# A gated mix of two S4 layers on one Trainium2 core: the last unit transposed on VectorE, one product per step in place of two, and a new written-out order

## The chip, the cores and the metric

The program runs on one core of a Trainium2 chip. The metric is device time in microseconds: the median of the runs shown. A core has four engines that compute, each with its own queue of instructions that it works off strictly in the order of the program: TensorE (PE in the profile, with PEld for the loading of its weights), VectorE (DVE), ScalarE (ACT) and GpSimd (POOL). SyncE (SP) issues all transfers of this kernel. [...] PSUM is the memory that TensorE writes its products to; SBUF holds everything else.

## The reference

Two state-space layers (A, "S4", and B, "S4D") see the same input `x` of 2048 steps by 512 channels. Each builds a convolution kernel of 2048 taps per channel from 128 complex exponentials, convolves the input with it through a Fourier transform of length 4096, and adds a skip term. A sigmoid gate, one number per step, mixes the two.

```python
x = A_u
g = _sigmoid((x * gate_w).sum(-1, keepdims=True))
# each layer: K[d,l] = Re sum_n C[d,n] * exp(dt*A[d,n]*l) * B[d,n]   (512 x 2048, 128 terms)
#             y = irfft(rfft(x, 4096) * rfft(K, 4096))[:2048] + x * Dskip
a = _A_ref(x, A_A_re, A_A_im, A_B_re, A_B_im, A_C_re, A_C_im, A_log_dt, A_Dskip)
b = _B_ref(x, B_log_A_real, B_A_imag, B_C_real, B_C_imag, B_log_dt, B_D_skip)
return g * a + (1 - g) * b
```

All is float32.

## The kernel before, in words

The 512 channels are cut into 4 quarters `q` of 128, and each quarter into 2 halves, which gives 8 units `v` of 64 channels, in both layers at once. A unit has two stages.

*Tables* (`tables`, `chunk`, eight chunks a unit): the 128 exponentials stand on the partitions. GpSimd makes angles (`near` L666, `turns` L657) and decaying amplitudes (`below` L677, `above` L685, into buffers `E`); ScalarE makes sine and cosine of the angles (L696 to L698, into the PSUM tiles `sd`); VectorE multiplies them (`sin 02` L702, `sin 1` L707, `cos 01` L712, `cos 2` L717); TensorE sums over the exponentials (`products`, L733, with the skip term at L743). One of ScalarE and VectorE copies the sums to `K` (L754), TensorE makes the first step of the Fourier transform (`put`, L775), and its result is copied to the large tile `F` (L787). The amplitudes of a unit come from a table `AB` that ScalarE fills with exponentials (`anchors`, L590 to L593, L607); the raw parameters of a quarter pass through a buffer of the same kind.

*Convolution* (`stage2`): for each of eight groups, TensorE makes the second step of the transform (`forward`, L797), VectorE multiplies the spectrum by that of the input (two instructions: `Z1` L868, by the real part, and `Z2` L871, by the imaginary part and a sign per partition), TensorE transforms back (L881), the result is copied to `st` (L884) and saved to HBM as `wt`. When both units of a quarter are done, `final` loads rows of `wt` (L1010), which turns the data since rows are read in another layout than they were saved in, TensorE makes the last step with the gate in its weights (L1021), and the result goes out (L1030).

The last unit, v = 7, has a way of its own: `stage2_half` does it in two halves `hf` of the channels with four groups each (`fwd half` L922, `Z1`/`Z2` L935 and L938, `back half` L946, a copy to `st` L953, a save L956), and `last` loads the rows of units 6 and 7 in pieces (L977), multiplies (`y`, L989), copies (L999) and sends out (L1000).

At the start VectorE computes exp(log_dt) in small steps on 128x8 numbers (L427 to L436), a matrix product spreads it (`spread`, L458), and the parameters of the first quarter follow; the input's own spectrum is made beside the first units (`stage1_u`, `stage2_u`) and saved to HBM as `ud` through buffers `z`.

The order of all of this is a list of numbers, `ORDER`, which names the 1920 steps in the sequence in which they are issued; each engine gets its own in that sequence. Buffers of a kind are handed out in the same sequence (`SLOTS` gives their number), so the list decides too which step waits for which buffer. `PICK` holds a bit for each copy that ScalarE or VectorE may do. `FILL` names places where TensorE gets matmuls whose result nobody reads (L299).

## Time and profile before

| | |
|---|---|
| median of 3 runs | 493.55 us (489.57, 493.55, 493.70) |
| the profiled execution | 488.42 us, its span 486.4 us |
| busy: DVE, PE, ACT, POOL | 412.6, 393.8, 386.5, 375.9 us |
| granted TensorE clock, mean | 0.956 |
| POOL's last amplitude | starts at 427.94 us |

The span is what the profile shows from the first to the last instruction; the execution's time has 2.0 us more around it. A row of a group reads: line, engine, operation, output<-input with shapes, number of instructions | busy microseconds, mean nanoseconds of one | idle microseconds just before them and who ended them. A row of the timeline reads: start, duration, engine, line, and in brackets the idle time before it. The windows give busy time for each engine in a stretch of the span, then the granted clock, the share of busy DMA and GB/s.

### The profile page before, as it was taken

How to read it: one execution, taken by the hardware profiler on the slowest of the kernel's cores; microseconds unless marked ns; L12 is line 12 of the kernel's file. 1: busy time of each engine (PE TensorE's matmuls, PEld its weight loads, DVE VectorE, ACT ScalarE, POOL GpSimd, SP SyncE). 2: the span in 40 equal slices, each digit the busy share in tenths (PEclk: the TensorE clock that was granted, in tenths of full speed). 3: DMA queues.
4: the chain of work that ended last, by engine and by line, in shares of the span. 5: the costliest groups of instructions: out<-in, count | busy, mean ns of one | idle time of the engine just before them, and what ended most of it. 6: DMA issues, size and time to landing. Idle time of an engine off the chain costs nothing.

```text
span 486.4 us, 23118 instructions
## 1 busy us (share of the span) xinstructions
PE 393.8 (81%) x10230; PEld 334.6 (69%) x10230; DVE 412.6 (85%) x614; ACT 386.5 (79%) x598; POOL 375.9 (77%) x333
## 2 busy tenths in 40 slices
PE   2987787979777879894779876789878899788895
PEld 2567666758666667783568765677767788687785
DVE  6998869997987999999999998999999999866500
ACT  4999978989987797889999989899999887571201
POOL 7588989995877999897589999889998999820000
PEclk9999989987998999999599999989999999998996
DMA  6247987663453445252145365556545447875683
GB/s 167 78 114 237 289 260 220 196 190 111 121 154 99 132 145 171 79 161 80 45 133 183 114 228 154 160 171 215 171 142 154 148 140 234 247 226 167 189 254 127
DMA packets 76503, 80.32 MB, mean 165 GB/s; under 512 B 13556, under 2 KB 58484, under 8 KB 76404
## 3 DMA queue, kind: packets, MB, share of 16 engines
q1 hardware_dynamic: 76404, 78.85, 53.6%
q8 instruction: 80, 1.31, 1.1%
q14 instruction: 19, 0.16, 0.1%
HBM read 45.25 MB, written 33.59 MB: 162 GB/s over the span
## 4 chain that ended last, share of the span: by engine, by line
PE 37%; ACT 22%; DVE 18%; issue 11%; POOL 6%; DMA 5%; SPq 1%; DVEq 0%; ACTq 0%; POOLq 0%
PE ps L797 8%; PE ps L733 6%; PE ps L775 6%; PE ps L881 5%; DVE QD L702 4%; PE sd L989 3%; PE ps L1021 3%; DVE E L712 3%; ACT sd L697 3%; ACT sd L696 2%; DVE z L871 2%; PE ps L922 2%; POOL E L685 2%; ACT AB L592 2%; PE ps L946 2%
## 5 line engine op out<-in xcount | busy, mean ns | idle before, releaser
L685 POOL TENSOR_TENSOR E<-AB 128x1024 f32<-128x1024 f32 x64 | 125.1, 1957 | 6.8 <-PE ps L733 6.6
L797 PE MATMUL ps<-F,Gw 128*128 128x128 f32 x576 | 84.3, 293 | 12.9 <-ACT st L884 5.4
L797 PEld LDWEIGHTS ps<-F,Gw 128*128 128x128 f32 x576 | 73.5, 199 | 25.1 <-ACT st L884 6.4
L702 DVE TENSOR_TENSOR QD<-sd,E 128x1024 f32<-128x1024 f32 x64 | 77.8, 1216 | 3.2 <-ACT sd L696 2.6
L712 DVE TENSOR_TENSOR E<-sd,E 128x1024 f32<-128x1024 f32 x64 | 77.8, 1218 | 2.0 <-ACT sd L698 0.8
L733 PE MATMUL ps<-E 128*32 128x64 f32 x2048 | 65.3, 225 | 15.9 <-DVE E L717 3.3
L677 POOL TENSOR_TENSOR E<-AB 128x512 f32<-128x512 f32 x64 | 68.0, 1069 | 12.2 <-PE ps L733 5.6
L657 POOL TENSOR_TENSOR x<-gh 128x512 int32<-128x512 int32 x64 | 68.0, 1068 | 10.7 <-ACT sd L697 6.1
L666 POOL TENSOR_TENSOR x<-pi,c_tm 128x512 int32<-128x512 int32 x64 | 67.7, 1060 | 8.2 <-DVE pi L478 6.9
L697 ACT ACTIVATE sd<-x 128x1024 f32<-128x1024 int32 x64 | 66.0, 1031 | 7.5 <-DVE E L712 3.2
L881 PE MATMUL ps<-z,Tw 128*64 128x128 f32 x896 | 61.8, 281 | 11.2 <-DVE z L871 4.2
L696 ACT ACTIVATE sd<-x 128x1024 f32<-128x1024 int32 x64 | 66.2, 1034 | 5.5 <-POOL x L657 1.3
L733 PE MATMUL ps<-QD 128*32 128x64 f32 x2048 | 64.8, 222 | 4.4 <-issue 4.4
L733 PEld LDWEIGHTS ps<-E 128*32 128x32 f32 x2048 | 50.0, 112 | 25.6 <-issue 11.7
L698 ACT ACTIVATE sd<-sd 128x1024 f32<-128x1024 f32 x64 | 64.4, 1006 | 1.7
L881 PEld LDWEIGHTS ps<-z,Tw 128*64 128x64 f32 x896 | 49.3, 138 | 19.7 <-DVE z L868 6.0
L733 PEld LDWEIGHTS ps<-QD 128*32 128x32 f32 x2048 | 52.1, 112 | 5.3 <-issue 5.2
L775 PE MATMUL ps<-w,K 64*64 64x64 f32 x2048 | 43.2, 225 | 11.1 <-issue 5.2
L775 PEld LDWEIGHTS ps<-w,K 64*64 64x64 f32 x2048 | 36.6, 137 | 22.5 <-issue 8.2
L707 DVE SCALAR_TENSOR_TENSOR QD<-sd,E 128x512 f32<-128x512 f32 x64 | 43.7, 683 | 4.2 <-POOL E L685 1.9
L717 DVE TENSOR_TENSOR E<-sd,E 128x512 f32<-128x512 f32 x64 | 43.7, 683 | 3.3 <-ACT sd L698 2.5
L871 DVE SCALAR_TENSOR_TENSOR z<-ps,sgn,U 128x512 f32<-128x512 f32 x56 | 41.4, 743 | 4.5 <-ACT sd L696 2.8
(153 smaller groups left out, 747.1 us busy)
## 6 DMA issues: line engine op xcount, KB each, us to landing
wt<-st SPq DMA_DIRECT2D x64, 256.0 KB, 3.2
U<-ud SPq DMA_DIRECT2D x28, 512.0 KB, 3.9
X<-wt SPq DMA_DIRECT2D x25, 512.0 KB, 4.8
ud<-z SPq DMA_DIRECT2D x24, 256.0 KB, 3.9
ud<-z SPq DMA_DIRECT2D x40, 128.0 KB, 3.4
U<-in_u SPq DMA_DIRECT2D x16, 256.0 KB, 3.4
U<-in_uT SPq DMA_DIRECT2D x8, 512.0 KB, 5.4
out<-st SPq DMA_DIRECT2D x16, 256.0 KB, 4.8
```

Of the source, the lines that this page charges most:

```text
L657: G.tensor_tensor(xi()[:, :, 1, :].rearrange("n c (a b) -> n c a b", a=4), t[:, :, 0:4].unsqueeze(3).to_broadcast([P, NCK, 4, 8]), t[:, :, ...
L666: lambda: G.tensor_tensor(xi()[:, :, 0, :], d["piv"]()[:, k, ch, 0].unsqueeze(2).to_broadcast([P, NCK, NJ]), tm[:, 0:NJ].unsqueeze(1).to_b ...
L677: G.tensor_tensor(Ev()[:, :, 0, :].rearrange("n c (a b) -> n c a b", a=4), A1()[:, ca, ::-1].unsqueeze(3).to_broadcast([P, NCK, 4, 8]), BB ...
L685: G.tensor_tensor(Ev()[:, :, 1:3, :].rearrange("n c w t -> n c (w t)"), AA()[:, ca].rearrange("n c w a -> n (c w) a").unsqueeze(3).to_broa ...
L696: op("A", "sin", lambda: A.activation(bv(sn), wv(xi()), AF.Sin, scale=SCL), r=[x], w=[sn])
L697: op("A", "abs", lambda: A.activation(bv(cs), wv(xi()), AF.Abs), r=[x], w=[cs])
L702: lambda: V.tensor_tensor(ev(QD)[:, :, 0::2, :], bv(sn).rearrange("n w c t -> n c w t"), Ev()[:, :, 0::2, :], ALU.mult),
L712: lambda: V.tensor_tensor(Ev()[:, :, 0:2, :], bv(cs)[:, 0].unsqueeze(2).to_broadcast([P, NCK, 2, NJ]), Ev()[:, :, 0:2, :], ALU.mult),
L733: T.matmul(K4[32 * b : 32 * b + 32, gg, :], ev(QD if w else E)[:, c, 2, :], ev(QD if w else E)[:, c, 0:2].rearrange("n h t -> n (h t)"), s ...
L775: T.matmul(bs[h].t[64 * d : 64 * d + 64, 64 * g : 64 * g + 64], K()[64 * h : 64 * h + 64, 64 * g : 64 * g + 64], w1[64 * h : 64 * h + 64, ...
L797: T.matmul(b.v("p (a m h e) -> p m a h e", a=4, m=4, h=16, e=2)[:, mm], Gw[:, m, :], Fv(F)[:, :, m, :].rearrange("p (a h) e -> p a h e", a=4),
L881: T.matmul(o[64 * i : 64 * i + 64], Tw[:, m, :], zv(z), start=True, stop=True)
```

## The change

- **One product per step.** `Z1` and `Z2` become one VectorE instruction of 128x1024 (`spread_mul`): the spectrum is read twice through a broadcast, against both parts of the input's spectrum, into one buffer `Z` (three of 1024). The sign moves into the weights `Tw` of the transform back, which are kept twice (`t sign`). Buffers `z` go from four to two and now serve the input's spectrum alone; tables `AB` go from three to two.
- **Last unit.** The results of `stage2_half` are no longer saved and read back. They are copied to SBUF (`tail`, half of an `F`, and for the second half the tile `X`), VectorE transposes them in 32x32 blocks (four instructions `turn`), and the last products (`y half`) use copies of the weights with their partitions in the matching order, which eight transfers from SBUF to SBUF make once (`perm`). Rows of unit 6 are still loaded (`rows`, four).
- **Start.** The small steps of exp keep their intermediate values in a PSUM bank (`exp_b`) where before all lay in SBUF.
- **Order.** `ORDER` (1851 steps), `PICK` and `FILL` are all new. Unread matmuls may now also be a repeat of a real step (`again`) or add zeros to a bank that is in use (`still`); counted in units of 128 columns there were 81 and there are 91.

On VectorE the first rows of the program were these, all of them between SBUF tiles (`ex_k`, `ex_r`, `ex_i` are the steps of exp):

```order
L427 TENSOR_SCALAR dt_t<-dt_t 128x8
L428 TENSOR_SCALAR ex_k<-dt_t 128x8
L429 TENSOR_SCALAR ex_k<-ex_k 128x8
L430 SCALAR_TENSOR_TENSOR ex_r<-ex_k,dt_t 128x8
L431 SCALAR_TENSOR_TENSOR ex_r<-ex_k,ex_r 128x8
L432 TENSOR_SCALAR dt_t<-ex_r 128x8
L434 SCALAR_TENSOR_TENSOR dt_t<-dt_t,ex_r 128x8 x7
```

Now, at the same place, each has a PSUM operand (`ps_104`):

```order
L433 TENSOR_SCALAR ps_104<-dt_t 128x8
L434 COPY dt_t<-ps_104 128x8
L435 TENSOR_SCALAR ps_104<-ps_104 128x8
L436 TENSOR_SCALAR ps_104<-ps_104 128x8
L437 SCALAR_TENSOR_TENSOR ex_r<-ps_104,dt_t 128x8
L438 SCALAR_TENSOR_TENSOR ex_r<-ps_104,ex_r 128x8
L439 TENSOR_SCALAR ps_104<-ex_r 128x8
```

One instruction is added (the copy), and none has two SBUF inputs any more.

At the end of the program VectorE had these rows behind its last copy to `F` (the last four groups of the second half of the last unit; `U` is the input's spectrum):

```order
L787 COPY F0_66<-ps0_101 128x8x64
L938 SCALAR_TENSOR_TENSOR z0_80<-ps2_103,sgn_123,U1_85 128x512
L935 TENSOR_TENSOR z2_82<-ps2_103,U1_85 128x512
L938 SCALAR_TENSOR_TENSOR z1_81<-ps3_104,sgn_123,U1_85 128x512
L935 TENSOR_TENSOR z3_83<-ps3_104,U1_85 128x512
L938 SCALAR_TENSOR_TENSOR z0_80<-ps1_102,sgn_123,U0_84 128x512
L935 TENSOR_TENSOR z2_82<-ps1_102,U0_84 128x512
L938 SCALAR_TENSOR_TENSOR z1_81<-ps3_104,sgn_123,U0_84 128x512
L935 TENSOR_TENSOR z3_83<-ps3_104,U0_84 128x512
```

Now it has four products and, around them, the four transposes:

```order
L806 COPY F0_66<-ps3_104 128x8x64
L985 STREAM_TRANSPOSE F1_67<-F1_67 128x32x32
L876 TENSOR_TENSOR Z0_81<-ps2_103,U0_84 128x1024
L876 TENSOR_TENSOR Z1_82<-ps3_104,U1_85 128x1024
L876 TENSOR_TENSOR Z2_83<-ps0_101,U1_85 128x1024
L876 TENSOR_TENSOR Z0_81<-ps1_102,U0_84 128x1024
L985 STREAM_TRANSPOSE F1_67<-F1_67 128x32x32
L985 STREAM_TRANSPOSE F1_67<-X_107 128x32x32 x2
```

Eight instructions of 512 became four of 1024; three of the four transposes stand last, behind every product.

SP's queue held near its end the saves of the last unit (`wt_109<-st`, L956) and the loads of the rows (L977):

```order
L956 DMA wt_109<-st1_87 128x8x64
L956 DMA wt_109<-st0_86 128x8x64
L977 DMA X_107<-wt_109 128x1024
L977 DMA X_107<-wt_109 128x512 x2
L977 DMA AB0_68<-wt_109 128x512
L977 DMA AB1_69<-wt_109 128x512
L977 DMA F1_67<-wt_109 128x512
L977 DMA AB1_69<-wt_109 128x1024
L1000 DMA out_0<-st1_87 128x512
```

Now it holds the last load of the input's spectrum (L944), copies of the weights (L1002) and rows of unit 6 (L888), and no save:

```order
L1002 DMA AB1_69<-wg_120 32x2048
L1075 DMA out_0<-st0_86 128x512
L888 DMA AB1_69<-wt_109 128x1024
L944 DMA U0_84<-ud_108 128x2x256
L888 DMA x1_71<-wt_109 128x1024
L1002 DMA AB1_69<-wg_120 32x2048
L888 DMA AB0_68<-wt_109 128x1024
L1002 DMA AB1_69<-wg_120 32x2048 x2
L888 DMA x0_70<-wt_109 128x1024
L1048 DMA out_0<-st0_86 128x512
```

The trip of the last unit through HBM is gone from the queue, and the last of the weights' copies stand close to the end.

```diff
-    "F": (4096, 2), "AB": (28 * NCH, 3), "x": (1024, 2), "E": (1536, 3), "QD": (1536, 2),
-    "K": (512, 2), "z": (512, 4), "U": (1024, 2),
+    "F": (4096, 2), "AB": (28 * NCH, 2), "x": (1024, 2), "E": (1536, 3), "QD": (1536, 2),
+    "K": (512, 2), "z": (512, 2), "Z": (1024, 3), "U": (1024, 2),
...
+    pl.still = lambda o, n: T.matmul(o, ident, tb[:, 1:2].to_broadcast([P, P * n]), start=False, stop=False)
...
+        op(
+            "A", "t sign", lambda: A.activation(Tw[:, 0], Tw[:, 1], AF.Copy, scale=sgn),
+            r=[(TwB, ((0, NJ), (1, 2), (0, 2))), sgnB], w=[(TwB, ((0, NJ), (0, 1), (0, 2)))],
+        )
...
+        x, k, y = (exp_b.t[:, 8 * i : 8 * i + 8].rearrange("p (a q) -> p a q", a=2) for i in range(3))
+        V.tensor_scalar(x, dt_t, -87.0, 88.0, ALU.max, ALU.min)
+        V.tensor_copy(dt_t, x)
...
+    def spread_mul(Z, b, U, mg):
+        u = U.v("p (w x n) -> p w x n", w=2, x=2, n=256)[:, :, mg % 2]
+        V.tensor_tensor(
+            Z.v("p (w k n) -> p w k n", w=2, k=2, n=256),
+            b.t.rearrange("p (k n) -> p k n", k=2).unsqueeze(1).to_broadcast([P, 2, 2, 256]),
+            u.unsqueeze(2).to_broadcast([P, 2, 2, 256]), ALU.mult,
+        )
...
-            op("V", "Z1", lambda Z1=Z1, b=b, uv=uv: V.tensor_tensor(m3(Z1.t), m3(b.t), uv(0), ALU.mult), r=[b, U], w=[Z1], hold=[Z2])
-            op(
-                "V", "Z2",
-                lambda Z2=Z2, b=b, uv=uv: V.scalar_tensor_tensor(m3(Z2.t), m3(b.t), sgn, uv(1), ALU.mult, ALU.mult),
-                r=[b, U, sgnB], w=[Z2],
-            )
+            op("V", "Z", lambda Z=Z, b=b, U=U, mg=mg: spread_mul(Z, b, U, mg), r=[b, U], w=[Z])
...
             op(
-                "D", "wt half",
-                lambda st=st, mg=mg: DMA(
-                    parts(v)[hf, 8 * mg : 8 * mg + 8].rearrange("m p c -> p m c"), st.v("p (m c) -> p m c", m=8, c=64)
+                "AV", "hb", lambda copy, hb=hb, mg=mg: copy(at()[:, 512 * mg : 512 * mg + 512], hb.t), r=[hb],
+                w=[sr(mg)], after=clear if hf else (),
+            )
+        for k in range(2):
+            op(
+                "V", "turn",
+                lambda k=k: V.transpose(
+                    tail.v("p (f s k c) -> p f k c s", f=2, s=NJ, k=2, c=32)[:, hf, k],
+                    at().rearrange("p (m k c) -> p k c m", k=2, c=32)[:, k],
                 ),
...
+        wa = [Buf("AB"), Buf("AB")]
+        for k in range(2):
+            for x in range(4):
+                op(
+                    "D", "perm",
+                    lambda k=k, x=x: DMA(
+                        wa[k].t[32 * x : 32 * x + 32, 0:2048], (wg if k else wb.t.rearrange("p (s c) -> p s c", c=64)).rearrange("(m x) s c -> x m (s c)", x=4)[x]
+                    ),
+                    r=[wgB], w=[(wa[k], ((x, x + 1),))], hold=[wb], after=ending,
+                )
...
+        for k in range(2):
             for bk in range(4):
...
+                    w = wa[k].t[:, 0:2048].rearrange("p (s c) -> p s c", c=64)
+                    tv = tail.v("p (f s k c) -> p s k f c", f=2, s=NJ, k=2, c=32)
+                    for a in range(4):
+                        for e in range(2):
+                            o0, s = 512 * (bk % 2) + 128 * a + 64, 8 * bk + 4 * e + a
+                            T.matmul(
+                                y.t[64 * e : 64 * e + 64, o0 : o0 + 64].rearrange("p (f c) -> p f c", f=2), w[:, s, :], tv[:, s, k],
+                                start=(k == 0 and a == 0), stop=(k == 1 and a == 3),
+                            )
```

More of the change, by code (lines that the diff above doesn't have):

```diff
@@ L212, in run @@
             done.add(o)
-            if k in FILL:
-                units, t, i = FILL[k]
-                for n in range(0, units, 4):
-                    m = min(4, units - n)
-                    self.keep(self.tiles[t][i][:, 0 : P * m].rearrange("p (k c) -> p k c", k=m), m)
+            for n, t, i in FILL.get(k, ()):
+                if t:
+                    self.keep(self.tiles[t][i][:, 0 : P * n].rearrange("p (k c) -> p k c", k=n), n)
+                elif i in self.again:
+                    self.again[i](n)
+                else:
+                    self.still(next(b for b in self.ops[i].bufs if b.tag == "ps").t[:, 0 : P * n], n)
             for b in o.bufs:
@@ L571, in params_c @@
         d["fi"] = fi
+    ending = []
     anch, step, Kt, kgs, first = {}, {}, {}, [None], [None]
@@ L601, in anchors @@
             op("A", f"exps{r0}", exps, r=[al], w=[(b, ((r0, r1),))], after=ones)
+            if v == NV - 1:
+                ending.append(pl.ops[-1])
         t = bank()
@@ L916, in stage2_half, with fwd @@
                     )
-            def fwd(mg=mg, b=b):
-                for mm in range(8):
+            def fwd(n=4, mg=mg, b=b):
+                for mm in range(2 * n):
                     m = 8 * mg + mm
```

226 lines of the change are left out of this document (111 added, 115 removed), and 194 rows, old and new, of tables (FILL, ORDER).

## The prediction

> **What bounds the kernel now.** I read the span on the page first, then busy time by windows, then the groups by line, and last the timeline of the first 25 and the last 60 us.
>
> ```profile
> span 486.4 us, 23118 instructions
> ```
>
> ```profile
> core 0: us, PE busy (x) PEld busy (x) DVE busy (x) ACT busy (x) POOL busy (x), PEclk, DMA share, GB/s
> 200.00:430.00 230.00, 189.06 (x5020) 163.38 (x5019) 218.75 (x329) 205.13 (x316) 207.05 (x171) 0.97 0.51 157
> 429.00:446.70 17.70, 13.90 (x437) 12.64 (x426) 12.22 (x18) 7.06 (x10) 0.00 (x1) 1.00 0.76 218
> 446.70:464.30 17.60, 15.65 (x428) 14.87 (x429) 7.34 (x11) 4.15 (x7) 0.00 (x0) 0.90 0.69 188
> 464.30:483.00 18.70, 15.98 (x389) 14.39 (x384) 0.00 (x0) 2.44 (x5) 0.00 (x0) 0.86 0.66 208
> ```
>
> There are two stages with different limits. In the steady part (200 to 430 us) VectorE is busy 218.75 of 230 us, 95%; GpSimd and ScalarE follow at 90% and 89%. VectorE is the first limit, but what it gives up the others allow only in part. From 429 on GpSimd is done, VectorE falls to nothing, and 57.4 us are left in which TensorE works through what remains, at a granted clock that sinks to 0.86, with the last unit's trip through HBM in between. A faster VectorE counts in the first stage; the removed trip counts in the second.
>
> **The change part by part.** *One product per step.*
>
> ```profile
> L868 DVE TENSOR_TENSOR z<-ps,U 128x512 f32<-128x512 f32 x56 | 38.0, 683 | 3.0 <-PE ps L797 1.4 <-PE ps L881 1.1 <-issue 0.3
> L871 DVE SCALAR_TENSOR_TENSOR z<-ps,sgn,U 128x512 f32<-128x512 f32 x56 | 41.4, 743 | 4.5 <-ACT sd L696 2.8 <-PE ps L797 1.5 <-ACT st L1029 0.2
> L702 DVE TENSOR_TENSOR QD<-sd,E 128x1024 f32<-128x1024 f32 x64 | 77.8, 1216 | 3.2 <-ACT sd L696 2.6 <-POOL E L677 0.3 <-POOL E L685 0.3
> L787 DVE COPY F<-ps 128x512 f32<-128x512 f32 x22 | 14.5, 684 | 3.2 <-PE ps L775 3.1
> L527 DVE RECIPROCAL AB<-p 128x256 f32<-128x256 f32 x4 | 7.0, 1746 | 0.0
> ```
>
> A step costs 683 + 743 = 1426 ns now. The new instruction has 1024 elements, one PSUM and one SBUF input, as L702 has: 1216 ns, with 2 x 683 = 1366 as the upper bound. That is 0.21 us a step (bounds 0.06 to 0.21), or 56 x 0.21 = 11.8 us off VectorE before the last unit. All of it would come off the span if VectorE alone set the pace. GpSimd at 90% and ScalarE at 89% are near behind: with VectorE at (218.75 - 7.9)/230 = 92% (the steady part holds about two thirds of the steps, 7.9 us), three engines of nearly equal load must fit, in a strict order, so I take half, -6 us, bounds 0 and -11.8. Nothing is added on TensorE: one weight load per matmul stays, from two copies of `Tw`. The sign's copy (128x2048 on ScalarE) replaces two of four half-height instructions there: zero.
>
> *Start.* VectorE's first instruction of 8 numbers takes as long as a GpSimd instruction beside it, and so do two more.
>
> ```profile
> 3.63 1.89 POOL L329 TENSOR_TENSOR x<-ints 128x1024 int32<-128x1024 int32 x1
> 3.65 1.90 DVE L427 TENSOR_SCALAR dt_t<-dt_t 128x8 f32<-128x8 f32 x1 [3.65 <-DMA dt_t<-in_log_dt]
> 5.58 0.22 DVE L428 TENSOR_SCALAR ex_k<-dt_t 128x8 f32<-128x8 f32 x1
> 5.99 1.89 POOL L329 TENSOR_TENSOR x<-ints 128x1024 int32<-128x1024 int32 x1
> 6.09 1.82 DVE L430 SCALAR_TENSOR_TENSOR ex_r<-ex_k,dt_t 128x8 f32<-128x8 f32 x1
> 8.07 1.89 POOL L329 TENSOR_TENSOR x<-ints 128x1024 int32<-128x1024 int32 x1
> 8.14 1.84 DVE L432 TENSOR_SCALAR dt_t<-ex_r 128x8 f32<-128x8 f32 x1
> 8.83 0.80 PE L299 MATMUL sd<-c_id 128*128 128x128 f32 x2 [0.77 <-DMA c_id<-in_c_id]
> 11.73 1.22 PE L458 MATMUL ps<-c_id,dt_t 128*128 128x128 f32 x4 [2.10 <-DVE dt_t L436]
> 22.60 1.06 POOL L666 TENSOR_TENSOR x<-pi,c_tm 128x512 int32<-128x512 int32 x1
> ```
>
> L427, L430 and L432 end within 0.03 us of the L329 beside them; L428, alone, takes 0.22. If the three fall to 0.22 the chain loses 1.90 + 1.82 + 1.84 - 0.66 = 4.9 us and gains one copy of 0.22: 4.7 less. The spread (11.73) would then wait until about 7.1 us for it; the identity matrix it also needs arrived just before 8.83, but its load stands earlier in the new queue. Behind the spread the parameters of the first quarter, then GpSimd's first table (22.60), are a chain on VectorE with copies in between, so part of it is used up there. I take -3, bounds 0 and -4.7. The row cannot say that a PSUM operand cures this. [...]
>
> *Last unit.* The rows that carry the end:
>
> ```profile
> 427.94 1.06 POOL L677 TENSOR_TENSOR E<-AB 128x512 f32<-128x512 f32 x1
> 431.83 1.16 PE L775 MATMUL ps<-w,K 64*64 64x64 f32 x64
> 446.47 0.39 PE L743 MATMUL ps<-dskip,c_id 128*128 128x8 f32 x2
> 446.79 1.93 PE L922 MATMUL ps<-F,Gw 128*64 128x64 f32 x32
> 463.09 1.15 PE L946 MATMUL ps<-z,Tw 128*64 128x64 f32 x32
> 464.07 0.29 PE L989 MATMUL sd<-F,X 128*64 128x64 f32 x4
> 469.36 1.35 PE L299 MATMUL ps<-c_id 128*128 128x512 f32 x4
> 482.90 0.58 ACT L999 COPY st<-sd 128x512 f32<-128x512 f32 x1 [3.82 <-PE sd L989]
> ```
>
> The timeline restricted to L989 gives the rate of the last products, and the list of transfers the trip that goes:
>
> ```profile
> 464.00:469.40 5.40, 4.97 (x160) 4.83 (x160) 1.00 0.91 242
> wt<-st SPq DMA_DIRECT2D x64, 256.0 KB, 3.2
> AB<-wt SPq DMA_DIRECT2D x4, 256.0 KB, 4.8
> ```
>
> From the tap that closes the last table (446.9) to the last product (482.8) pass 35.9 us. In the new order TensorE has behind that tap 7 groups of `back half`, 4 of `fwd half`, one `put`, 128 last products (it was 192) and 768 unread columns. That is 11 x 1.15 + 1.16 = 13.8; the products are 256 instructions at 4.97/160 = 0.031, 8.0; the columns 768 x 1.35/640 = 1.6. Sum 23.4 us of work. Waits: `K` and `F` are copied once each before the first forward group (0.68 a copy), covered by three groups of `back half`; behind the last `back half` come a copy (0.58) and the transpose on which the first `y half` rests, covered by half of the products with unit 6 (64 instructions, 2.0 us) and the first unread matmul. I allow 2.5 us for both, and 1 for a clock below full: 27, so 9 less. The stretch from 429 to 446.9 has nearly the same work on TensorE in both orders and 3.8 us of waits; I take 1 of it. The tail is -10.
>
> What was late was the data's trip: 3.2 + 4.8 = 8 us from a copy to the rows. What comes next is the transpose, whose price this trace does not hold. The nearest rows by shape are L787, 684 ns for 512 elements, which gives 1.37 for 1024, and by far above it the reciprocal, 1746 ns for 256, which gives 7.0. I take 1.4, since it moves and does not divide; three of the four stand last, so 5.6 us a piece more would cost 11 to 12 us. [...] The bounds of the tail are -4 (only the 64 products and half of the waits go) and -16 (no wait is left, and 429 to 446.9 loses its 3.8).
>
> The copies of the input's spectrum into `z` and the transfers of `z`, from the view of that tile:
>
> ```profile
> L830 DVE COPY z<-ps x18: 681/686/693, 31.7 to 142.1; 128x512 f32<-128x512 f32 x18
> L830 ACT COPY z<-ps x14: 567/588/636, 41.2 to 156.1; 128x512 f32<-128x512 f32 x14
> DMA to landing us min/median/max: 1.7/3.5/6.4
> ```
>
> *Fewer tables and buffers `z`; the order; unread matmuls.* I cost these at zero. Cover for the tables is the distance in the order: the exponentials of the next unit stand while GpSimd still has chunks of the current one, as before. Two `z` where there were four hold the input's spectrum only; a copy (0.68) and a save's landing (median 3.5 below) make 4 to 5 us for a buffer, so a pair passes 32 results in 80 us, and they now spread over some 125 (below: L830 starts between 31.7 and 156.1). If this cover fails here and there, up to 5 us.
>
> **The sum.** -6 - 3 - 10 = -19 on the span: 467.4, and 469.4 with the 2.0 us around it. The profiled execution (488.42) is the fastest of four; their mean deviates by 2.9 us from it ((0 + 1.15 + 5.13 + 5.28)/4). A median of new runs I put at 469.4 + 2.9 = **472 us**, 4.4% under 493.55.
>
> **The rivals.** *VectorE was not the limit.* GpSimd (207 of 230) and ScalarE (205) take its place, the body gains nothing, the start one: 488.4 - 1 - 10 + 2.9 = 480. For it speak the nearly equal loads; against it VectorE's short waits (L868 and L871 together 7.5 us in the whole program).
>
> *The first `y half` is late.* A transpose nearer to 7 us, or copies of the weights (eight transfers of 256 KB) that land behind it: 12 us given back, 472 + 12 = 484. The rows of L787 speak against it.
>
> *Slower: two tables `AB`.* A unit's exponentials must wait until the last amplitude of the unit but one has been made, and if ScalarE gets to them late, GpSimd stands still at each change of unit.
>
> ```profile
> L592 ACT ACTIVATE AB<-al 128x256 f32<-128x256 f32 x32 | 15.8, 640 | 0.0
> L591 ACT ACTIVATE AB<-al 128x256 f32<-128x256 f32 x24 | 12.2, 637 | 0.0
> L593 ACT ACTIVATE AB<-al 128x128 f32<-128x128 f32 x32 | 9.2, 444 | 0.0
> L590 ACT ACTIVATE AB<-al 128x128 f32<-128x128 f32 x32 | 9.1, 440 | 0.0
> L677 POOL TENSOR_TENSOR E<-AB 128x512 f32<-128x512 f32 x64 | 68.0, 1069 | 12.2 <-PE ps L733 5.6 <-ACT AB L592 2.5 <-ACT z L830 2.3
> ```
>
> The four make 46.3 us for eight units, 5.8 a unit; six changes exposed in full cost 35: 472 + 35 = 507. To be slower by 1% (above 498.5) takes 26.5 us, nearly five changes in full. Against it: with three tables GpSimd waited 2.5 us for them in all, and the order places them early.
>
> *The new order gives it all back.* Engines that wait in line for others lose about as much as is saved, here and there, by in-order waits and a lower clock: 488 to 494.
>
> **How the numbers follow.** A difference under 1% is what a measurement of this kernel can't tell from none, since its own runs spread by 0.8%. Chances: forecast 0.62 (459 to 479), VectorE not the limit 0.16, late `y half` 0.07, two tables 0.07, all given back 0.08. Range: the bounds of the terms together would be 488.4 - 11.8 - 4.7 - 16 = 456 and 488.4 - 0 - 0 - 4 + 5 = 489; all ends seldom meet, so 459 to 487, which leaves out the last two cases and a little below. Faster by over 1% (under 488.6): the first two and most of the third, 0.83. Within 1%: the rest of it and the case of all given back, 0.10. Slower: 0.07.
>
> **What would show it.** Right: the one product at 1.2 us in 64 instances and VectorE's sum near 405 us (412.6 - 64 x 0.21 + 4 x 1.4); the first steps of exp all near 0.2 us and the spread at 7 to 9 us; a transpose near 1.4 us; about 27 us from the last tap to the last product and about 46 from GpSimd's end to the end of the span; GpSimd's end near 420. Wrong: GpSimd ending at 428 or later with ScalarE or table waits before it (first rival or third), a transpose of several us, or a gap in front of the first `y half`.

## The result and the profile after

The changed kernel takes 475.31 us (median of 472.21, 474.93, 475.68 and 479.06) against 493.62 for the kernel before on the same chip: a ratio of 0.966, with a 95% interval of 0.956 to 0.976. (Some executions of a kernel are over 1.5% longer than its fastest; the medians here count them, the ratios and their intervals leave them out.) The profiled execution is the shortest of the four, the one of 472.21 us, with a span of 470.2 us at a mean granted clock of 0.955 (before: 486.4 at 0.956), so 16.2 us have gone from the span. The forecast was 472.0, with 459 to 487. The sum came out nearly right; its terms did not, and two of the errors cancel.

**Where the time went.** GpSimd's long amplitudes, 64 instructions of one form in each kernel, make a clock that can be read in both. First the timeline of GpSimd before, restricted to that form: the 1st, the 32nd and the last of the 64.

```profile
29.25 1.95 POOL L685 TENSOR_TENSOR E<-AB 128x1024 f32<-128x1024 f32 x1
...
225.04 1.96 POOL L685 TENSOR_TENSOR E<-AB 128x1024 f32<-128x1024 f32 x1
...
426.03 1.95 POOL L685 TENSOR_TENSOR E<-AB 128x1024 f32<-128x1024 f32 x1
```

The same three in the changed kernel:

```profile
23.31 3.87 POOL L695 TENSOR_TENSOR E<-AB 128x1024 f32<-128x1024 f32 x2 [6.29 <-ACT AB L601]
...
211.13 1.97 POOL L695 TENSOR_TENSOR E<-AB 128x1024 f32<-128x1024 f32 x1
...
413.44 1.97 POOL L695 TENSOR_TENSOR E<-AB 128x1024 f32<-128x1024 f32 x1
```

The lead is 5.9 us at the first, 13.9 at the 32nd and 12.6 at the last. The gain is made before 225 us. In the second half, the steady part that the prediction built on, the changed kernel is not faster at all: 202.3 us against 201.0, though at a lower granted clock (0.94 against 0.97, in the rows below). The windows of both say the same (columns as in the prediction: length, busy time of TensorE, its weight loads, VectorE, ScalarE, GpSimd, granted clock, DMA share, GB/s). Before:

```profile
184.90:225.00 40.10, 34.70 (x1037) 30.06 (x1038) 39.38 (x54) 33.17 (x47) 38.57 (x33) 1.00 0.43 128
225.00:426.00 201.00, 164.16 (x4270) 141.28 (x4269) 191.06 (x291) 179.57 (x279) 180.58 (x150) 0.97 0.52 160
```

After, the same two stretches of work and then the two parts of the tail, from GpSimd's end to the last tap and from there to the last product:

```profile
175.00:211.10 36.10, 30.04 (x791) 25.98 (x795) 34.91 (x43) 32.60 (x43) 36.02 (x30) 0.95 0.45 136
211.10:413.40 202.30, 175.72 (x4396) 151.74 (x4386) 188.28 (x256) 181.29 (x284) 181.95 (x152) 0.94 0.56 169
415.40:433.80 18.40, 14.85 (x466) 13.46 (x467) 11.10 (x12) 6.64 (x10) 0.01 (x1) 1.00 0.86 216
433.80:466.70 32.90, 23.80 (x677) 21.68 (x676) 16.10 (x12) 5.20 (x9) 0.00 (x0) 0.90 0.53 131
```

In the steady half VectorE's busy time fell from 95.1% to 93.1% and the pace stayed. From the 25th to the 32nd amplitude VectorE had been busy 39.38 of 40.1 us; there it has 4.5 us less to do (43 instructions instead of 54), and 4.0 us are gained.

The groups by line price the two new operations, the one product and the transpose (`turn`):

```profile
L876 DVE TENSOR_TENSOR Z<-ps,U 128x1024 f32<-128x1024 f32 x64 | 77.2, 1218 | 14.6 <-PE ps L954 7.1 <-PE ps L818 4.2 <-ACT sd L707 1.3
...
L985 DVE STREAM_TRANSPOSE F<-F 128x1024 f32<-128x1024 f32 x2 | 4.5, 2249 | 1.0 <-ACT F L979 1.0
L985 DVE STREAM_TRANSPOSE F<-X 128x1024 f32<-128x1024 f32 x2 | 4.4, 2218 | 0.0
```

The product costs 1218 ns, as forecast (1216). The transpose costs 2.2 us, not 1.4.

The start, from the timeline of its first 11 us:

```profile
3.64 1.90 POOL L335 TENSOR_TENSOR x<-dtb 128x1024 int32<-128x1024 int32 x1
3.67 1.42 DVE L441 SCALAR_TENSOR_TENSOR ps<-ps,ex_r 128x8 f32<-128x8 f32 x7
...
7.03 1.19 PE L465 MATMUL ps<-c_id,dt_t 128*128 128x128 f32 x4 [7.03 <-DMA c_id<-in_c_id]
```

Seven steps of the exponential run beside a GpSimd instruction of 1.9 us and take 0.20 each. The spread starts at 7.03 instead of 11.73, and what it waits for now is the identity matrix.

The tail shows the surprise. TensorE's timeline from the last tap to the last product:

```profile
433.41 0.39 PE L753 MATMUL ps<-dskip,c_id 128*128 128x8 f32 x2
...
438.45 0.67 PE L954 MATMUL ps<-F,Gw 128*64 128x64 f32 x13
445.71 5.19 PE L954 MATMUL ps<-F,Gw 128*64 128x64 f32 x115 [6.59 <-issue]
...
465.49 1.15 PE L1034 MATMUL sd<-F,AB 128*64 128x64 f32 x32 [0.96 <-ACT st L1047]
```

After 13 of the 128 matmuls of `fwd half` TensorE stands still for 6.59 us, in the middle of a group that waits for a semaphore at its first matmul alone. "issue" means that nothing in the profile holds it. Tap to last product is 32.8 us where 27 were forecast. In that time the DMA engines are nearly full, as the view of transfers from 425 to 450 us shows (88.4% is the data's share of 16 engines' time; the last number of an issue line is the median us from issue to landing):

```profile
q1 hardware_dynamic: 2149, 5.04, 88.4%
q8 instruction: 4, 0.07, 1.1%
...
AB<-wg SPq DMA_DIRECT2D x4, 256.0 KB, 12.4
...
x<-wt SPq DMA_DIRECT2D x2, 512.0 KB, 10.2
```

Among 5.04 MB of data go four transfers of instructions. Their queue, q8, carries packets of 16 KB, one every 5.3 us in the median of this run. Between the one that starts at 432.42 us and the next there are 10.0 us. The view of transfers from 442 to 443 us shows that next one, which starts at 442.46 and takes 1.45 us:

```profile
q1 hardware_dynamic: 40, 0.15, 88.5%
q8 instruction: 1, 0.02, 9.1%
```

It has landed at 443.91, and TensorE goes on at 445.71. So the theory for the experiments: TensorE ran out of instructions, and the next block stood behind the `rows` and the copies of the weights (`perm`).

### The profile page after: what moved, and what is told of

It is laid out like the page before. It is cut to its first block, busy times and chain, and to the rows that moved or that the text cites. A ratio compares the mean times of both kernels' runs of the same rounds, so it can differ in the third digit from the quotient of the medians.

```text
span 470.2 us, 22888 instructions
## 1 busy us (share of the span) xinstructions
PE 391.2 (83%) x10154; PEld 334.5 (71%) x10154; DVE 407.6 (87%) x556; ACT 384.0 (82%) x596; POOL 375.2 (80%) x332
## 4 chain that ended last, share of the span: by engine, by line
PE 30%; DVE 23%; ACT 21%; issue 11%; DMA 9%; POOL 4%; SPq 1%; DVEq 1%; ACTq 0%; POOLq 0%
PE ps L818 7%; PE ps L912 6%; PE ps L743 5%; DVE QD L712 5%; PE ps L785 4%; DMA ud<-z 4%; DVE Z L876 4%; ACT sd L706 4%; DVE E L722 3%; ACT sd L707 3%; PE ps L1066 3%; DVE E L727 2%; DVE QD L717 2%; PE ps L954 2%; ACT L706 2%
## 5 line engine op out<-in xcount | busy, mean ns | idle before, releaser
L695 POOL TENSOR_TENSOR E<-AB 128x1024 f32<-128x1024 f32 x64 | 125.3, 1962 | 10.8 <-ACT AB L601 6.3
L818 PE MATMUL ps<-F,Gw 128*128 128x128 f32 x618 | 90.6, 292 | 11.4 <-ACT F L806 2.8
L818 PEld LDWEIGHTS ps<-F,Gw 128*128 128x128 f32 x618 | 78.2, 197 | 22.1 <-issue 5.1
L876 DVE TENSOR_TENSOR Z<-ps,U 128x1024 f32<-128x1024 f32 x64 | 77.2, 1218 | 14.6 <-PE ps L954 7.1
L912 PE MATMUL ps<-Z,Tw 128*64 128x128 f32 x896 | 62.8, 286 | 9.3 <-DVE Z L876 4.7
L912 PEld LDWEIGHTS ps<-Z,Tw 128*64 128x64 f32 x896 | 50.4, 141 | 16.2 <-DVE Z L876 5.7
L785 PE MATMUL ps<-w,K 64*64 64x64 f32 x2048 | 41.8, 222 | 9.8 <-issue 2.9
```

The lines of the kernel that those rows point to most:

```text
L695: G.tensor_tensor(Ev()[:, :, 1:3, :].rearrange("n c w t -> n c (w t)"), AA()[:, ca].rearrange("n c w a -> n (c w) a").unsqueeze(3).to_broa ...
L785: T.matmul(bs[h].t[64 * d : 64 * d + 64, 64 * g : 64 * g + 64], K()[64 * h : 64 * h + 64, 64 * g : 64 * g + 64], w1[64 * h : 64 * h + 64, ...
L818: T.matmul(b.v("p (a m h e) -> p m a h e", a=4, m=4, h=16, e=2)[:, mm], Gw[:, m, :], Fv(F)[:, :, m, :].rearrange("p (a h) e -> p a h e", a=4),
L876: V.tensor_tensor(Z.v("p (w k n) -> p w k n", w=2, k=2, n=256), b.t.rearrange("p (k n) -> p k n", k=2).unsqueeze(1).to_broadcast([P, 2, 2, ...
L912: T.matmul(o[64 * i : 64 * i + 64], Tw[:, i, m, :], Z.v("p (w a m c) -> p w m a c", w=2, a=4, m=4, c=32)[:, i, mm], start=True, stop=True,)
```

## The experiments

Each run has its ratio to the kernel before on the same chip, since chips and hours differ (before: medians of 489.2 to 493.9 us). The last column is the stretch from GpSimd's end to the end of the span in the profiled execution. It is the steadiest measure of the tail, because GpSimd's end itself lies anywhere between 413 and 424 us in kernels with the same instructions up to there. Kernels with the same tail differ in it by up to 2 us (54.8 and 55.8, 46.4 and 48.3), so less than that is not resolved.

| run | median us | ratio to before (95%) | GpSimd's end to end of span, us |
|---|---|---|---|
| before | 493.6 | 1 | 57.4 |
| changed kernel | 475.3 | 0.966 (0.956 to 0.976) | 54.8 |
| no weight copies | 468.2 | 0.953 (0.943 to 0.962) | 49.2 |
| 32 x + m, one transfer for rows | 529.0 | 1.077 (1.068 to 1.086) | 54.1 |
| two products | 477.9 | 0.972 (0.964 to 0.981) | 55.2 |
| exp steps in SBUF | 479.7 | 0.969 (0.956 to 0.983) | 54.1 |
| late copies | 472.4 | 0.964 (0.957 to 0.971) | 52.1 |
| rows by quarter | 466.5 | 0.952 (0.944 to 0.960) | 46.4 |
| no unread matmuls | 474.7 | 0.967 (0.955 to 0.979) | 54.8 |
| turn layouts | 474.8 (one) | - | 53.2 |
| four `z` | 471.3 | 0.957 (0.950 to 0.965) | 55.8 |
| best, turned | 467.9 | 0.948 (0.940 to 0.955) | 49.4 |
| copies back | 479.9 | unclear | 54.6 |
| best, four `z` | 469.6 | 0.970 (0.961 to 0.979) | 48.3 |

Within a kernel, runs at a higher granted clock are shorter: one slope for all kernels, fitted to the 60 runs that the comparisons use, is 2.2 us (1.5 to 2.9) for 0.01 of clock. Differences "at equal clock" below are those of that fit, with its 95% bounds. It takes all chips and hours as one. The kernel before alone lies 13.0 to 16.6 us above the changed kernel at equal clock, depending on the chip and hour, so a difference of 3 us or less can be theirs.

### The stop in the tail

**No copies of the weights.**

```
- wa[k].t[32 * x : 32 * x + 32, 0:2048], (...).rearrange("(m x) s c -> x m (s c)", x=4)[x]
+ wa[k].t[32 * x : 32 * x + 1, 0:2048], (...).rearrange("(m x) s c -> x m (s c)", x=4)[x, 0:1]
```

> The eight copies of the weights (`perm`, L1002, 256 KB each) are cut to one partition of 32 each (8 KB); the rest of the copied weights is left out, so the products of the last unit use stale numbers. Nothing else changes: same order, same instructions on every computing engine. Theory (instruction supply): TensorE's stop of 6.59 us in the middle of the `fwd half` group at 439.12 is a transfer of instructions that stands behind the copies and rows in the DMA engines; with 2 MB less traffic it goes, or falls under 1.5 us: last tap to last product 26 to 28 us instead of 32.8, end 5 to 6.5 us earlier, 469 to 470. Rival 1 (the rows' transfers alone suffice, or the stop does not depend on traffic): a stop of 5 us or more stays within the groups of `fwd half` or `back half`, 474 to 476. Rival 2 (something else is late next, such as the transposes of 2.2 us): the stop goes, but the last products wait instead, 472 to 474.

468.16 us, 5.4 us (2.5 to 8.3) less than the changed kernel at equal clock. TensorE's timeline at the same place:

```profile
437.80 0.68 PE L954 MATMUL ps<-F,Gw 128*64 128x64 f32 x13
442.32 6.14 PE L954 MATMUL ps<-F,Gw 128*64 128x64 f32 x115 [3.84 <-issue]
```

The stop is at the same instruction, 13 into the group, and shorter: 3.84 instead of 6.59. The `rows`, which were left, keep part of it. So both the theory and the first rival hold in part: traffic sets its length, and not the copies alone. The same stop, with 114 or 115 matmuls still to go, is in all the other runs with this TensorE stream: 5.77 us with two products, 6.05 with the steps in SBUF, 5.77 with the turn layouts, 4.12 with four `z`. Without the unread matmuls the stream is shorter, and the stop (5.79) falls elsewhere in `fwd half`. A place fixed in the instruction stream with a length that varies with the traffic is what a block of instructions that comes late looks like. The packets in the traces bear it out. Here the block on q8 lands at 441.06 us, and the stop ends at 442.32. In the 14 traces of this case there are 140 stops of TensorE of over 0.5 us behind the first 20 us that are put down to "issue", and 136 of them end 1.1 to 1.9 us after such a packet has landed. A moment picked at random lies there in 14 of 100 cases.

**Late copies.** Three copies and one `rows` go to ScalarE's queue, behind two copies `hb`.

```
+ nc.scalar.dma_start for three perm and the last rows; in ORDER behind the first and second hb
```

> The whole result, the same transfers. Three of the eight copies of the weights and the last of the four `rows` of unit 6 are issued from ScalarE's queue, behind the first and the second copy `hb` of the last half, instead of from SP between 435 and 438 us: 1.25 MB less stands in the DMA engines while TensorE is in the `fwd half` groups. Theory (the stop in `fwd half` is instruction supply behind a burst of transfers): the stop of 6.59 us falls to 3 us or less (it was 3.84 without any copies of the weights), and the late transfers land beside the last unit's inverse, before 461: 470 to 473. Rival 1: the moved transfers land behind the first `y half` or `y` that needs them, which waits as long as the stop was: 474 to 478. Rival 2: the stop stays at 6 us: 475.

472.43 us. The stop shrinks to 3.30, a little above the 3 expected, and a wait for the moved copies appears before the last products:

```profile
441.88 5.38 PE L960 MATMUL ps<-F,Gw 128*64 128x64 f32 x114 [3.30 <-issue]
...
457.64 1.15 PE L1040 MATMUL sd<-F,AB 128*64 128x64 f32 x32 [1.50 <-DMA AB<-wg]
```

The tail is 2.7 us shorter by its stretch. The time, 2.6 us less at equal clock, is within its bounds (-5.7 to 0.5). The direction agrees; the size is not settled.

**No copies, and the whole result.** The transpose leaves the last unit on partition 32 x + m, while weights and `rows` are on 4 m + x; that is why the weights are copied. If all `rows` and the weights are laid out as 32 x + m, one set of weights serves both, and `wr` can go to `w1i` without its trip through HBM.

```
- wt_t[v].rearrange("m (x s) c -> (m x) s c", x=4)[:, 8 * bk : 8 * bk + 8]
+ bass.AP(wt_t.tensor, wt_t[v].offset + 1024 * bk, [[4096, 4], [16384, NJ], [1, 1024]])
- w = wa[k].t[:, 0:2048].rearrange("p (s c) -> p s c", c=64)
+ w = ws()[k]
```

> The whole result is computed, with no copy of the weights at all: the weights and all rows of the inverse transform are put on the partitions in the order in which the transpose leaves the last unit (32 x + m instead of 4 m + x), so that the same weights serve both. The eight copies and the small trip of `w1i` through HBM go; the rows' transfers keep their pieces of 4 KB in another order. Theory (instruction supply behind the copies): as without the copies, the 6.59 us stop goes and the time falls by 5 to 7 us, to 468 to 470. Rival: the stop stays, 474 to 476; or the reordered rows land later than 5 to 10 us and the last products wait for them, 475 to 480.

528.98 us, slower than either kernel: a miss that neither side of the expectation had at this size. The `rows` came late: TensorE waited 24.9 us for them in four places. While one of them is under way, the window of this run shows

```profile
261.00:268.00 7.00, 4.49 (x153) 3.74 (x152) 6.20 (x7) 5.23 (x8) 7.00 (x6) 1.00 0.27 94
```

and the changed kernel, at the same `rows`,

```profile
255.00:260.00 5.00, 3.77 (x141) 3.13 (x139) 5.00 (x6) 4.97 (x6) 5.00 (x4) 1.00 0.92 339
```

The new pattern's outermost dimension is 4, where it was 128. By estimate the share of 0.27 is 4.3 of the 16 engines that it is a mean of; that the pattern leaves 4 at work is read from this number alone, and how a transfer is divided among the engines is not shown.

**Rows by quarter.** The same layout, each `rows` as four transfers of 32 partitions.

```
+ for x in range(4):
+     DMA(f[32 * x : 32 * x + 32].rearrange("p (s c) -> p s c", s=8),
+         wt_t[v].rearrange("m (x s) c -> x m s c", x=4)[x, :, 8 * bk : 8 * bk + 8])
```

> As the run in which rows and weights were put on the partitions in the order 32 x + m, without copies of the weights, the whole result computed. The one difference: each `rows` transfer of 128 partitions is made by four transfers of 32 partitions (one for each x), so that no transfer has an outer dimension of 4. SP issues 84 transfers more, at some 0.41 us each 34 us of its time. Theory (in the run before, the outer dimension of 4 left only 4 of the 16 DMA engines at work, 80 to 130 GB/s, and every `rows` landed late): the transfers go at full rate again, TensorE's waits for `rows` (25 us) go, and the time falls below the changed kernel's, 468 to 473. Rival (SP becomes late: eight issues of 0.41 us ahead of each `y`, everything behind them in the queue 2.5 us later, 24 times): 478 to 490.

466.51 us, a ratio of 0.952, and 7.6 us (4.7 to 10.5) less than the changed kernel at equal clock: faster than both. SP's 84 more issues cost nothing that shows. TensorE's timeline from the tap on has no stop for "issue", and its blocks of instructions come without a gap of over 7 us:

```profile
429.89 0.39 PE L753 MATMUL ps<-dskip,c_id 128*128 128x8 f32 x2
...
433.93 1.15 PE L971 MATMUL ps<-Z,Tw 128*64 128x64 f32 x32
434.93 5.03 PE L955 MATMUL ps<-F,Gw 128*64 128x64 f32 x128
439.98 4.64 PE L971 MATMUL ps<-Z,Tw 128*64 128x64 f32 x128
...
454.99 0.64 PE L1033 MATMUL sd<-F,wg 128*64 128x64 f32 x16
```

Tap to last product is 25.3 us, and GpSimd's end to the end 46.4.

**Copies back.** The same kernel with the eight copies at their old places in the queue, read by nobody.

```
- lambda: None, r=[wgB], w=[(wa[k], ((x, x + 1),))],
+ lambda k=k, x=x: DMA(wa[k].t[32 * x : 32 * x + 32, 0:2048], ...), r=[wgB], w=[(wa[k], ((x, x + 1),))],
```

> The kernel with `rows` by quarter, with the eight copies of the weights (256 KB each) put back at their old places in the queue, though nothing reads them. The result stays whole; every computing engine has the same instructions as without them. Theory (the stop of 6.59 us in the changed kernel is TensorE's instruction supply behind these transfers): a stop of 3 to 7 us for `issue` comes back in a group of `fwd half` after the last tap, at the same instruction (13 matmuls into a group), and the time rises from 466.5 by 3 to 7 us: 470 to 473. Rival (it was the form of the `rows` transfers, or their place, that took the stop away): no stop over 1.5 us, 466 to 468.

The tail goes back to 54.6 us, and a stop comes back, not in `fwd half` but in front of the last matmul of `back half`:

```profile
454.57 3.94 PE L971 MATMUL ps<-Z,Tw 128*64 128x64 f32 x127
462.34 0.27 PE L971 MATMUL ps<-Z,Tw 128*64 128x64 f32 x1 [3.82 <-issue]
```

The expected place was wrong: TensorE's stream in this layout has other waits in it, so by my reading its blocks end elsewhere (two other runs in this layout without the copies have short stops one matmul before the end of `fwd half`, 0.39 and 0.20 us). The stop has the expected size, and it ends 1.4 us after its block has landed. The tail grew by 8.2 us. Of these, stops of over 0.5 us for "issue" make 5.1 (7.4 against 2.3 in the rows by quarter), and the granted clock there was 0.92 against 1.00. The time of 479.9 us is higher than expected, because GpSimd's end, which no copy can move (the first is issued 4 us behind it), was 10.6 us later in this profile than in the kernel without them. Its four executions took 472.1 to 484.7 us, of which the shortest alone lies in the expected range; the ratio is unclear, and only the tail is used here.

The runs above show that TensorE's stops end 1.1 to 1.9 us after a packet of instructions has landed (136 of 140), and that the stop in the tail is longer with more traffic in the DMA engines; a wait for a block of instructions is the reading that fits both. The copies are not most of it: with the `rows` in one piece and no copies the stop was 3.84 us, with the copies and the `rows` by quarter 3.82, with both as in the changed kernel 6.59. Why the block comes late behind such traffic is not shown by any run.

### The start and the products

**Exp steps in SBUF.** Same order, the three intermediate numbers in an SBUF tile.

```
- x, k, y = (exp_b.t[:, 8 * i : 8 * i + 8]...
+ x, k, y = (ex_s[:, 8 * i : 8 * i + 8]...
```

> The intermediate numbers of the exponential of dt (x, k, y; 8 numbers a partition each) lie in SBUF again instead of a PSUM bank; order and instructions stay. Theory (a VectorE instruction with its operands in SBUF waits for the GpSimd instruction beside it): up to 3.64 us nothing changes, from there, beside the GpSimd additions of 1.9 us each (L335), some steps take 1.8 us instead of 0.17, three or four of them, and the spread starts at 11 to 13 us instead of 7.03; at the end of the program 0 to 4.7 us of it are left, forecast 3: 475 to 480. Rival (the gain came from the load of dt that now stands first in the queue): all steps stay near 0.17 us, the spread at 7, time unchanged.

The timeline of the start:

```profile
3.73 1.82 DVE L440 TENSOR_SCALAR ex_s<-ex_r 128x8 f32<-128x8 f32 x1
5.59 4.78 DVE L442 SCALAR_TENSOR_TENSOR ex_s<-ex_s,ex_r 128x8 f32<-128x8 f32 x7
6.00 3.75 POOL L335 TENSOR_TENSOR x<-dtb 128x1024 int32<-128x1024 int32 x2
...
10.71 1.23 PE L466 MATMUL ps<-c_id,dt_t 128*128 128x128 f32 x4 [10.71 <-DVE dt_t L444]
...
27.05 1.96 POOL L696 TENSOR_TENSOR E<-AB 128x1024 f32<-128x1024 f32 x1 [6.31 <-ACT AB L602]
```

The waits are back: one step takes 1.82 and seven take 4.78 instead of 1.42. The spread is 3.7 us later and the first amplitude also 3.7 (27.05 against 23.31). The rival falls: an early load of dt is not what made the steps short. Of the lead of 5.9 us at the first amplitude, 3.7 are the PSUM bank's; the rest is left for the early load and the order, which no run separates. At the end the time is 0.8 us more at equal clock, within -2.7 and 4.3, so how much of the 3.7 survives to the end is not resolved.

**Two products.**

```
- V.tensor_tensor(Z (w k n), b to_broadcast [P, 2, 2, 256], u to_broadcast [P, 2, 2, 256], ALU.mult)
+ V.tensor_tensor(zv[:, 0], bv, u[:, 0], ALU.mult)
+ V.scalar_tensor_tensor(zv[:, 1], bv, 1.0, u[:, 1], ALU.mult, ALU.mult)
```

> The new order and everything else stay, but each step's product is again made by two VectorE instructions of 512 elements (a plain product and one with a scalar of 1.0, the forms of before: 683 and 743 ns) instead of one of 1024 (1217 ns). VectorE gets 64 x 0.209 = 13.4 us more work, of which some 11 us stand before GpSimd's end. Theory (VectorE is the first limit, GpSimd and ScalarE close behind: half of it shows): GpSimd's last instruction ends 6 us later (421 instead of 415.4), 481 to 483. Rival 1 (VectorE was not the limit): 475 to 477. Rival 2 (VectorE alone sets the pace): all of it, 487 to 489.

The two instructions, in the groups by line of this run:

```profile
L878 DVE TENSOR_TENSOR Z<-ps,U 128x512 f32<-128x512 f32 x64 | 43.7, 683 | 17.5 <-PE ps L953 6.4 <-PE ps L818 4.5 <-ACT st L919 2.9
L879 DVE SCALAR_TENSOR_TENSOR Z<-ps,U 128x512 f32<-128x512 f32 x64 | 43.5, 679 | 0.0
```

With an immediate number in place of the column `sgn` the second form costs 679 ns and not 743, so the pair is 10 us more work on VectorE (87.2 against 77.2), not 13.4. The time is 2.7 us more at equal clock (-0.2 to 5.6). That VectorE alone sets the pace, and all 10 us show, is excluded; that half of them show, or none, is not. GpSimd's end came at 421.3, as the theory said (421), but kernels with one product reach it anywhere from 413 to 424. Its steady half, from the 32nd to the last amplitude, took 202.7 us (216.6 to 419.3), against 202.3 in the changed kernel at the same granted clock of 0.94, and 201.2 to 207.0 in all ten profiles with one product and unread matmuls (the 32 x + m run with late `rows` left out): no worth of the merging shows there. From the 1st to the 32nd amplitude it took 192.9 us, against 187.8 in the changed kernel but 186.9 to 193.4 in the ten, so the early half does not settle it either.

### What was costed at zero

**No unread matmuls.**

```
- for n, t, i in FILL.get(k, ()):
+ for n, t, i in ():
```

> All unread matmuls (FILL) of the changed kernel are left out, nothing else; the result stays whole. Theory (they only keep TensorE's clock up and fill gaps): the mean granted clock falls below 0.94, and where TensorE sets the pace, at the start and in the tail, it costs 2 to 6 us: 477 to 481. Rival (their work on TensorE is worth as much as the clock): 474 to 476. If the tail is 2 us shorter without the two in front of the last products, they were no cover but a cost.

474.70 us: the forecast loss did not come. There is no difference in the time, but two that cancel. The window from 74 to 125 us of this run:

```profile
74.00:125.00 51.00, 43.16 (x1130) 37.96 (x1125) 43.41 (x70) 43.51 (x75) 37.30 (x32) 0.84 0.55 167
```

The same window of the changed kernel:

```profile
74.00:125.00 51.00, 41.24 (x1144) 34.61 (x1137) 45.67 (x72) 46.20 (x77) 41.04 (x36) 1.00 0.59 177
```

Without the unread matmuls the granted clock sinks to 0.84, and the 16th amplitude is 5.3 us later (130.0 against 124.7). From the 32nd to the last it is 4.5 us quicker (197.8 against 202.3). At equal clock the run is 4.1 us faster (1.0 to 7.2): they pay for themselves through the clock and no more. The tail is 54.8 us with and without.

**Four `z`.** For the copies `z` until the third `Z` is needed, its halves serve as two more buffers.

```
+ pl.tiles["z"] += [pl.tiles["Z"][2][:, 512 * i : 512 * i + 512] for i in range(2)]
```

> The changed kernel with four buffers `z` while the input's spectrum is made: the two more are the halves of the third buffer `Z`, handed to `z` only before the point in the order where `Z` needs it. Order and instructions stay. Theory of the forecast (two buffers cost nothing): GpSimd's last instruction ends within 2 us of the changed kernel's 415.4, 473 to 476. Rival (the chain of waits of the changed kernel has 4.4% of transfers `ud<-z` between 38 and 82 us, so these buffers do hold the start back): the copies into `z` end earlier than 149.1, GpSimd's end comes 3 to 8 us earlier, 467 to 472.

A ratio of 0.957, whose interval overlaps the changed kernel's, and 4.1 us (1.1 to 7.2) less at equal clock. But the profile (of an execution of 477.9 us) gives it no place to come from: the 16th amplitude is at 125.3 (124.7 in the changed kernel), the copies into `z` run until 152.5 (149.1), and GpSimd's end is at 420.1 (415.4), earlier in none of them as the rival would have it. The transfers `ud<-z` in the chain of waits were a way through the start, not a limit. Together with the rows by quarter:

> The whole result: `rows` by quarter, no copies of the weights, the transposes as in the changed kernel, and four buffers `z` for the input's spectrum as in the run with four. Theory (the two add up, the buffers being worth 0 to 4 us): 463 to 466.5, a ratio of 0.943 to 0.952. Rival (four buffers are worth nothing, their ratio of 0.957 was the spread of the runs): 466 to 469, 0.951 to 0.955.

469.62 us, a ratio of 0.970, no better than the rows by quarter alone, and 2.5 us more at equal clock. The gain of the run before did not come again: the rival holds as far as these runs go, four buffers are worth nothing that two runs agree on, and costing two at zero was right within some 4 us.

### The transpose

**Turn layouts.** Four patterns for the four instructions; the last unit's output is misplaced by three of them.

```
  "p (f s k c) -> p f k c s"  (out, steps of 64)   or  "p (f s k c) -> p f k s c"  (32 neighbours)
  "p (m k c) -> p k c m"      (in, steps of 64)    or  "p (m k c) -> p k m c"      (32 neighbours)
```

> The four transposes of the last unit are given four different patterns over the same 1024 elements and the same memory: (1) as in the changed kernel, both sides with steps of 64 elements (256 bytes); (2) input in steps, output with 32 neighbouring elements; (3) input with 32 neighbouring elements, output in steps; (4) neighbouring elements on both sides. The last unit's numbers are put in the wrong places by (2) to (4); time is all that is asked. [...]

The view of this line (shortest, median, longest ns; each pair holds two layouts, in order of time the longer first in both):

```profile
L985 DVE STREAM_TRANSPOSE F<-F x2: 2021/2096/2172, 443.3 to 457.0; 128x1024 f32<-128x1024 f32 x2
L985 DVE STREAM_TRANSPOSE F<-X x2: 1187/1584/1982, 459.1 to 461.0; 128x1024 f32<-128x1024 f32 x2
```

Steps on both sides (1) took 2.17 us, on the input alone (2) 2.02, on the output alone (3) 1.98, on neither (4) 1.19. So the steps make it slow, and (2) and (3) do not lie halfway: steps on one side are enough, and mending one side buys 0.2.

**Best, turned.** Neighbours on both sides, on top of the rows by quarter; the copies `hb` write, and the last products read, in steps of 128 bytes.

```
+ copy(at().rearrange("p (k c m) -> p k c m", k=2, c=32)[:, :, :, 8 * mg : 8 * mg + 8], ...)
+ tv = tail.v("p (f k c s) -> p s k f c", f=2, k=2, c=32, s=NJ)
```

> The whole result. The kernel with `rows` by quarter and no copies of the weights (466.5 us), and the transposes of the last unit with neighbouring elements on both sides: the copies `hb` write their 512 elements in steps of 128 bytes, the last products read the transposed tile in steps of 128 bytes. Theory: each transpose takes 1.2 us instead of 2.2 (1187 ns with neighbours on both sides), two of the three behind the last `hb` stand on the path, so 2 to 3 us come off: 463.5 to 464.5. Rival (the steps cost the copies or the products as much as the transposes save): copies `hb` over 0.8 us instead of 0.59, or the groups of 32 last products over 1.5 us instead of 1.15: 466 to 468.

467.86 us, a ratio of 0.948 that cannot be told from 0.952. From the groups by line of this run:

```profile
L1036 PE MATMUL sd<-F,X 128*64 128x64 f32 x64 | 4.1, 288 | 0.7 <-ACT st L1049 0.7
...
L989 DVE STREAM_TRANSPOSE F<-F 128x1024 f32<-128x1024 f32 x2 | 2.5, 1241 | 1.0 <-ACT F L980 1.0
L989 DVE STREAM_TRANSPOSE F<-X 128x1024 f32<-128x1024 f32 x2 | 2.4, 1224 | 1.3 <-ACT X L980 1.3
L980 ACT COPY X<-ps 128x512 f32<-128x512 f32 x4 | 2.3, 587 | 7.7 <-DMA x<-wt 6.4 <-PE ps L971 1.3
```

The transposes fall to 1.2 us and the copies stay at 587 ns, but the last products slow down: a group of 32 takes 1.97 us instead of 1.15, and the one thing new in these products is that their moving columns lie in steps of 128 bytes. That is 0.8 us for each of four times 32, 3.3 in all, against 3 saved on the three transposes. The granted clock was 1.00 for these products in both runs. The rival holds.

## Why the prediction was right, and where it was not

**One product per step: price right, worth not found where it was put.** 1218 ns against 1216. I put half of the 11.8 us on the path, because VectorE at 95% seemed the first limit of the steady part. That step failed: the steady half did not become faster when VectorE fell to 93.1%, nor, within the 6 us by which equal kernels differ there, slower when two products brought its busy time back to 191.29 us. For that half the first rival (VectorE was not the limit) is borne out. Between the 25th and 32nd amplitude VectorE was at 98%; it had 4.5 us less to do there, of which the eight products are 1.7, and 4.0 us were gained. That the products did this is not shown: with two products this stretch took 37.2 us, in the ten profiles with one 36.1 to 37.8.

**The order, costed at zero.** The lead grows by 8.0 us between the 1st and the 32nd amplitude. That is a favourable pair of profiles: before took 195.8 us for this stretch, the ten with one product 186.9 to 193.4. Two products change the whole time by 2.7 (-0.2 to 5.6), so the merging is hardly all of it. No run kept the old order with the new product, so how the 8.0 divide between the merging and the places of the instructions stays open. That the body came out 6 to 8 us shorter in this profile, near the forecast of 6, is luck: it was gained ahead of the steady part, in which most of it was forecast, and in the quickest of four executions.

**Start: right, too small.** The steps are short and the spread came at 7.03, in the forecast's 7 to 9. I took 3, so I expected 1.7 of the 4.7 us to be used up on the way; the lead at the first amplitude is 5.9, of which 3.7 are shown to be the PSUM bank's. Beside a GpSimd instruction of 1.9 us a step with a PSUM operand took 0.20 us; with the numbers in SBUF one step took 1.82 and seven 4.78. Which operands make a step wait is not shown: L440 of that run has a single SBUF input and took the 1.82 us. GpSimd's end came at 415.4, not near 420.

**Tail: the term that failed, -2.6 instead of -10.** The sum of TensorE's work was sound: 25.3 us from tap to last product in the rows by quarter, where all of it is done without the copies, against 27 forecast. What I left out was the supply of TensorE's own instructions. "I allow 2.5 us for both, and 1 for a clock below full" should have had a third wait, of 6.6 us, behind a queue that the change itself fills: eight copies of 256 KB beside four `rows` of 512 KB. (Before, the longest stop of this kind behind 425 us was 1.94 us.) I had those copies in a rival (they land behind the first `y half`), and looked at who reads them, not at who shares the engines with them. The window from GpSimd's end to the last tap had a DMA share of 0.76 before, in a row that I quoted. The rest of the error, 1.5 us, lies ahead of the tap: from GpSimd's end to the tap it took 18.4 us, where I had put 16.9.

**Transpose: 1.4 taken, 2.2 measured.** I took twice a copy's 684 ns for 512 elements (L787), which counts elements and leaves out the steps between them. Neighbouring elements on both sides come in below that (1.19 us), steps of 256 bytes on both sides far above it (2.17). Why steps cost so much is not shown by any run. Three of the four transposes stand last and took 0.8 us more each than I had put, so by estimate this is worth 2.4 us of the tail at most.

**The other rivals.** Two tables `AB` did not make GpSimd stand still: it waited 6.3 us for them at its first amplitude and 3.8 once more ahead of 226 us, and not at each change of unit. Two `z` cost nothing that two runs agree on. "All given back" did not happen. Added up on the span: -13.6 up to GpSimd's end, against -9, and -2.6 behind it, against -10, make -16.2 against -19.

## What to carry to other kernels

A burst of transfers in front of the last stage can go with a stop of an engine in a group that reads none of it (here 6.59 us of TensorE): look in the timeline for a stop in the middle of a group, with "issue" as its cause, and compare it with the DMA share of the same window and with the times at which packets of instructions land. Before copying data to fit a layout that an operation leaves behind, see whether the other side of the product can be laid out that way from the beginning, and look at the outermost dimension of each transfer (here a DMA share of 0.27 at 94 GB/s went with 4 and of 0.92 at 339 GB/s with 128, and with 32 no wait of TensorE for `rows` was left in the tail). An engine at 95% is the limit only where the pace follows when its work changes, so price a saving stage by stage, and check which of the cancelling terms the result has really confirmed.

## What the runs showed of the hardware

- TensorE stopped for up to 6.59 us at an instruction fixed in its stream, while data took 88.4% of the DMA engines' time; with the copies gone 3.84, with the `rows` in smaller transfers too, none. The stop ended 1.80 us after a packet of 16 KB of instructions had landed, and 136 of 140 stops in all traces ended 1.1 to 1.9 us after one. Beside the stop of 6.59 us, 5.04 MB of data and four such packets moved in 25 us.
- A copy of 256 KB from SBUF to SBUF landed after 12.4 us (median of four) in that traffic.
- While transfers with an outermost dimension of 4 were under way the DMA share was 0.27 at 94 GB/s, against 0.92 at 339 GB/s beside the same transfers with 128 outermost.
- A matmul whose 64 moving columns lie 128 bytes apart took 288 ns against 225 in the run that reads neighbours, and a group of 32 took 1.97 us against 1.15, both at a granted clock of 1.00.
- The same kernel's time moved by some 2.2 us for each 0.01 of granted clock. Kernels with the same instructions up to GpSimd's end reached it anywhere from 413 to 424 us, which is more than most of the effects asked for here; a stretch of the trace with fixed ends (GpSimd's end to the end) told them apart where the whole time did not.
